# Pooled-query scores with 64 weight columns per matmul, and attention's list of work laid out anew

## Chip, cores and metric

The kernel runs on one core of one Trainium2 chip. The metric is device time in microseconds (us), the median of three runs. The engines are TensorE (PE in the rows; PEld is its weight loads, which overlap the matmuls), VectorE (DVE), ScalarE (ACT), GpSimd (POOL) and SyncE (SP), which here issues the loads and stores.

## What is computed

Attention through 32 pooled queries p, a mixture of experts in which each token goes to one expert, and a gated two-matrix layer, all in fp32:

```python
def sm_attn(qq, kk, vv):                       # scale = 1/sqrt(64)
    s = scale * np.matmul(qq, kk.transpose(0, 1, 3, 2))
    s = s - np.max(s, axis=-1, keepdims=True)
    a = np.exp(s)
    a = a / (np.sum(a, axis=-1, keepdims=True) + 1e-09)
    return np.matmul(a, vv)
p_packed = sm_attn(p, k, v)                    # 8 batches, 8 heads, 32 x 576, d = 64
out = sm_attn(q, p_packed, p_packed)           # 576 x 32: the pooled-query scores
...
logits = xn @ en.T / tau                       # 4608 rows, 8 experts
expert_idx = np.argmax(logits, axis=1)
...
h = np.maximum(x[mask] @ w1[e], 0.0)
out[mask] = gate_w[mask, None] * (h @ w2[e])
...
a = x @ w_a
b = x @ w_b
return (a * b @ w_out).astype(np.float32)
```

## The kernel before

The program has three stages, one after the other: attention (to about 196 us), the experts (lines 823 to 1135), and the gated layer with an output by quadrants (from line 1235). The change is in attention alone.

Attention goes by batch. `prep(b)` loads p, k and v; k and v come in halves of four heads (tiles `k` and `v`, three buffers each, 576 KB a load). It transposes p (L248) and k (L268), makes the scores of p with k (L298, L303), the maximum, the exponential (L323) and its sum, transposes these (L352), and adds up the pooled values with v (L369) in PSUM tile `sm`. They are scaled (L386), transposed (L394) and kept as `ppT`, two tiles with heads side by side. From them come the small products `gr` (L408 to L413). `query(b)` loads q in halves, transposes it (L453) into five tiles `qT`, and runs three windows of 192 queries by `rest`: the pooled-query scores `s2_mm` (L491), maximum (L497), subtraction (L501), exponential (L505), sum and reciprocal (L509, L510), norm (L514, on GpSimd or VectorE), transposes (L520), the products with `gr` that give norms and expert logits (L534), and two sums (L543, L548). When a batch's windows are done, `experts` chooses each token's expert by a chain of small VectorE operations (L667), in whose middle a square root is taken on GpSimd (L696).

In `s2_mm` the weights are columns of `qT` (128 rows, two positions by 64), and the moving operand is 32 or 64 columns of `ppT`. Each matmul takes 32 weight columns, so four of them fill the 128 partitions of the result: 32 matmuls a window, 24 windows. An fp32 matmul is two rows of the trace, each with a weight load.

The order of all this isn't written by hand. `Sched` gets a list of operations: the engines each may run on with a duration in us, its dependencies, a priority, the buffers it takes and frees, and `lat`, the time until others may use its result. `run` goes through it with a clock for each engine, takes among the operations that could start within 0.05 us of the earliest the one with the lowest priority number, puts it on the engine on which it would end first, and calls its code. The durations so set the order on each engine and which engine makes a copy; they are no time that anything waits. On the chip each engine runs its own list in that order and waits only for data and buffers. "D" is the load queue: SyncE's, in the order of the list. The copies out of PSUM are all line 202 (ScalarE) or 204 (VectorE).

The end of attention's plan is handed to the plan of the experts as its starting clocks; the third stage has a plan of its own.

Of the kernel before, what the change touches and what calls it, by code (L numbers as in the profile page):

```python
# [18 lines left out]
B, H, S, D, NP, E = 8, 8, 576, 64, 32, 8  # L19
# [5 lines left out]
QA = 1.5  # L25
NB = 0.6
EN0 = 5.0


class Ctx:  # L30
# [118 lines left out]
NW = CI // 3  # L149


def attention(ctx, tc, c, q, k, v, p, a_dram, pT_dram, consts, more):
    nc = tc.nc
# [50 lines left out]
            nc.vector.tensor_copy(out=out, in_=in_)  # L204

    def evict(n):
        return {"A": 0.12 + 0.0009 * n, "V": 0.1 + 0.00105 * n}

    t_en = Buf("tr")
    o_en = op({"T": 0.33}, en_mm, take=[t_en], prio=-4.0, start=EN0)  # L210
# [3 lines left out]

    def halves(x, b, h):
        return x[b, 4 * h:4 * h + 4].rearrange("(m h) (p i) d -> (h p) m (i d)", h=2, i=CI)

    def prep(b):
        lo, hi = (first[b - 1] - AHEAD, first[b] - AHEAD) if b else (-8.0, -1.0)
# [16 lines left out]
        o_p = op({"D": 0.2}, load_p, prio=at(-1.0), take=[bp], lat=2.0)  # L236
        o_k, o_v = [], []
        for l, f, pr, bb in ((o_k, load_k, -0.75, bk), (o_v, load_v, -0.45, bv)):
            for h in range(2):
                l.append(op({"D": 1.7}, f(h), deps=l[-1:], prio=at(pr) + 0.04 * h, take=[bb[h]], lat=2.0))  # L240


        def pT_mm(e):
# [42 lines left out]
        for g in range(2):  # L286
            def s1_mm(a, g=g):
                def f(e):
                    ps = psum("tr", ("s1p", b, g, a))
                    if (g, a) == (0, 0):  # L290
                        tile_("e", ("e", b), [128, CI, 2, D])

                    def w(j):
                        h = 2 * j + g
                        return T_["pT", b][:, h // 4, a, h % 4 * 32:h % 4 * 32 + 32]

                    for j in range(4):
                        nc.tensor.matmul(  # L298
                            ps[32 * j:32 * j + 32, 0:256].rearrange("q (i p) -> q i p", i=4), lhsT=w(j),
                            rhs=T_["kT", b, j][:, :, 64 * g:64 * g + 64], start=True, stop=True)  # L300
                    if a == 0:
                        for j in range(4):
                            nc.tensor.matmul(  # L303
                                ps[32 * j:32 * j + 32, 256:320], lhsT=w(j),
                                rhs=T_["kT", b, 4][:, j, 64 * g:64 * g + 64], start=True, stop=True)
                return f

            def s1_ev(a, g=g):
                def f(e):
                    s = (slice(0, 5), slice(5, 9))[a]  # L310
                    n = s.stop - s.start
                    copy(e, T_["e", b][:, s, g], T_["s1p", b, g, a][:, 0:n * D].rearrange("p (i q) -> p i q", i=n))
                return f

            def mx(e, g=g):
                T_["mx", b, g] = m = st.tile([128, 1], F32, tag="mx1", name="mx1")
                nc.vector.tensor_reduce(out=m, in_=T_["e", b][:, :, g], axis=AX.XY, op=ALU.max)
                nc.vector.tensor_scalar(out=m, in0=m, scalar1=-0.125, scalar2=None, op0=ALU.mult)

            def exp(e, g=g):  # L320
                T_["sm", b, g] = sm = st.tile([128, 1], F32, tag="sm1", name="sm1")
                ee = T_["e", b][:, :, g]
                nc.scalar.activation(  # L323
                    out=ee, in_=ee, func=AF.Exp, bias=T_["mx", b, g], scale=0.125, accum_out=sm)

            def rs(e, g=g):
                T_["rs", b, g] = r = st.tile([128, 1], F32, tag="rs1", name="rs1")
                nc.vector.tensor_scalar(out=r, in0=T_["sm", b, g], scalar1=1e-9, scalar2=None, op0=ALU.add)
                nc.vector.reciprocal(out=r, in_=r)

            f = lambda x, g=g: at(x + 0.1 * g)
            evs = []
            for a in range(2):
                t = Buf("tr")
                o = op({"T": 0.62}, s1_mm(a), deps=[o_pT] + o_kT, prio=f(0.25), take=[t] if g + a else [t, be],
                       free=[bpT] + bkT[0:4] + ([] if a else bkT[4:]))
                evs.append(op(evict(288), s1_ev(a), deps=[o], prio=f(0.25), free=[t]))
            o = op({"V": 0.86}, mx, deps=evs, prio=f(0.33))
            o = op({"A": 0.76}, exp, deps=[o], prio=f(0.37))
            T_["rso", b, g] = op({"V": 0.27}, rs, deps=[o], prio=f(0.55))  # L340
            o_e.append(o)

        def chunk(i):
# [31 lines left out]
        mms = []  # L375
        for i0, i1 in ((0, 4), (4, 8), (8, 9)):
            t = Buf("tr")
            o = op({"T": 0.11 * (i1 - i0)}, eT_mm(i0, i1), deps=o_e, prio=at(0.45 + 0.01 * i0),
                   take=[t] if i0 else [t, beT], free=[be])
            o = op(evict(128 * (i1 - i0)), eT_ev(i0, i1), deps=[o], prio=at(0.45 + 0.01 * i0), free=[t])  # L380
            mms.append(op({"T": 0.25 * (i1 - i0)}, pp_mm(i0, i1), deps=[o] + o_v + mms[-1:], prio=at(0.6 + 0.01 * i0),
                          take=[] if i0 else bs, free=[beT] + bv))

        for g in range(2):
# [42 lines left out]
            o = op({"V": 0.26}, ppx_ev, deps=[T_["rso", b, g]] + mms, prio=f(0.75), take=[bc], free=[bs[g]])  # L427
            o = op({"T": 0.11}, ppT_mm, deps=[o], prio=f(0.8), take=[t, bT], free=[bc])
            ppT_ops[b, g] = [op({"A": 0.17, "V": 0.2}, ppT_ev(a), deps=[o], prio=f(0.8), free=[t]) for a in range(2)]
            t = Buf("tr")  # L430
            o = op({"T": 0.35}, gr_mm, deps=ppT_ops[b, g], prio=f(0.9), take=[t], free=[bT])
            o = op({"V": 0.21}, gr_ev, deps=[o], prio=f(0.9), take=[bx], free=[t])
            gr_ops[b, g] = op({"A": 0.06, "V": 0.08}, m8_ev, deps=[o], prio=f(0.9), free=[t])
            c.kept[b, g] = op({"D": 0.4}, keep, deps=ppT_ops[b, g], prio=f(1.0), free=[bT], lat=2.0)

    x_ops = {}
# [1 line left out]
    def query(b):  # L438
# [2 lines left out]
        at = lambda x: first[b] + x  # L441
        o_q = []
        for h in range(2):
            o_q.append(op({"D": 1.7}, lambda e, h=h: nc.sync.dma_start(
                out=turn("q", ("q", b, h))[:, :, 0:CI, :].rearrange("p m i d -> p m (i d)"), in_=halves(q, b, h)),
                prio=at(-3.2 + 0.3 * h), deps=o_q[-1:], take=[bq[h]], lat=2.0))
        o_qT, bqT = [], []
        for x in range(5):
            def qT_mm(e, x=x):
# [24 lines left out]
    def rest(b, w, o_qT, bqT, before):  # L474
# [10 lines left out]
        def s2_mm(e):  # L485
            ps = psum("sm", ("s2", t))[:, 0:384].rearrange("p (i j k) -> p i j k", i=3, j=4)
            for j in range(4):
                for i, n in runs:
                    for o in range(0, 128, 32):
                        pT = T_["ppT", b, o // 64][:, j]  # L490
                        nc.tensor.matmul(  # L491
                            ps[o:o + 32, i - 3 * w:i - 3 * w + n, j], lhsT=T_["qT", b, i // 2][:, j, o:o + 32],
                            rhs=pT if n == 2 else pT[:, i % 2, :].unsqueeze(1), start=True, stop=True)

        def mx(e):
# [51 lines left out]
        def add(e):  # L547
# [2 lines left out]
        B_ = {n: Buf(n) for n in ("a", "an", "sq", "sm")}  # L550
        f = lambda x: 1.5 * t + x
        used = sorted({i // 2 for i, _ in runs})
        o = op({"T": 0.95}, s2_mm, deps=[o_qT[x] for x in used] + ppT_ops[b, 0] + ppT_ops[b, 1], prio=f(0),
               take=[B_["sm"]], free=[bqT[x] for x in used] + [T_["bppT", b, g] for g in range(2)])
        o = op({"V": 0.46}, mx, deps=[o], prio=f(0))
        o = op({"V": 0.47}, sub, deps=[o], prio=f(0), take=[B_["a"]], free=[B_["sm"]])
        o = op({"A": 0.43}, exp, deps=[o], prio=f(0))
        o = op({"V": 0.72}, total, deps=[o], prio=f(0.2))
        o = op({"V": 0.47} if t >= NW * B - 2 else {"P": 0.9, "V": 0.47}, norm, deps=[o], prio=f(0.2),
               take=[B_["an"]], free=[B_["a"]], bias={"V": NB})  # L560
        tr = Buf("tr")
        o = op({"T": 0.33}, aT_mm, deps=[o], prio=f(0.5), take=[tr], free=[B_["an"]])
        o_T = op(evict(384), aT_ev, deps=[o] + before[:1], prio=f(0.5), take=[] if w else [T_["baT", b]], free=[tr])
        x = Buf("x")
        o = op({"T": 0.8}, x_mm, deps=[o_T, gr_ops[b, 0], gr_ops[b, 1]], prio=f(0.7), take=[x],
               free=[T_["baT", b], T_["bgr", b, 0], T_["bgr", b, 1]])
        o_d = op({"A": 0.15, "V": 0.1}, dots, deps=[o], prio=f(0.8), free=[x])
        o = op({"V": 0.5}, sq, deps=[o], prio=f(0.8), take=[B_["sq"]], free=[x, B_["an"]])
        o = op({"V": 0.46}, add, deps=[o], prio=f(1.5), free=[B_["sq"]])
        x_ops[b] = x_ops.get(b, []) + [o_d, o]  # L570
        return o_T

# [99 lines left out]
def experts(nc, c, pool, b, psum):  # L672
# [36 lines left out]
    def g():  # L709
# [1151 lines left out]
```

## Time and profile before

| | us |
|---|---|
| median of 3 runs | 1387.64 |
| lowest and highest | 1387.16, 1387.8 |
| the profiled execution | 1386.53 |
| its span, first to last instruction | 1384.8 |

| engine | busy us | share of the span |
|---|---|---|
| TensorE matmuls | 1333.1 | 96% |
| TensorE weight loads | 1212.8 | 88% |
| VectorE | 799.1 | 58% |
| ScalarE | 589.7 | 43% |
| GpSimd | 106.9 | 8% |

The shares are means over stages that differ: the second and third stage keep TensorE full, attention doesn't. Matmuls overlap, so a busy TensorE isn't one at its peak. A gap that is put down to "issue" is one in which the engine waited for nothing that the profile shows. Windows are in us from the first instruction.

### The profile page before, as it was taken

Reading aid. Unit: us, or ns where it says so; the run is one execution under the profiler, and the core shown is the slowest. Engines: PE = TensorE matmul, PEld = TensorE weight load, DVE = VectorE, ACT = ScalarE, POOL = GpSimd, SP = SyncE. Lnnn points to the kernel's source line nnn. Section 1 sums busy time; section 2 is a strip of 40 time slices with the busy share of each in tenths; the row PEclk is TensorE's granted clock in tenths of the full one; section 3 lists DMA queues with packets and bytes.
Section 4 is the critical chain, followed back from the end, with each engine's and each line's share of the span. In section 5 each row is a group of like instructions: output and inputs, shape, how many; then the busy total and the mean of one; then the engine's idle time right before and its main releaser. Section 6 shows DMA issues by size and latency. Waiting matters only on the chain. (4 is left out here: it accounts for less than half of the span.)

```text
span 1384.8 us, 28211 instructions
## 1 busy us (share of the span) xinstructions
PE 1333.1 (96%) x11031; PEld 1212.8 (88%) x11031; DVE 799.1 (58%) x1644; ACT 589.7 (43%) x1212; POOL 106.9 (8%) x235
## 2 busy tenths in 40 slices
PE   7988879999999999999999999999999999999997
PEld 5766768999999999899999998999999989999996
DVE  4877875666766664888563446344634463444342
ACT  4655533444544444555442344234423442343232
POOL 1111210101001010000010001000100010001001
PEclk9999999999999999999999999999999999999999
DMA  7777446888676843777765566556765665556552
GB/s 266 232 253 244 155 154 203 278 265 286 227 248 197 282 148 131 256 257 255 256 196 162 158 204 199 161 158 201 209 161 159 193 209 162 158 167 199 161 158 66
DMA packets 169277, 278.14 MB, mean 201 GB/s; under 512 B 16936, under 2 KB 68520, under 8 KB 169136
## 3 DMA queue, kind: packets, MB, share of 16 engines
q1 hardware_dynamic: 162704, 257.35, 60.3%
q0 software_dynamic: 6272, 18.88, 3.9%
q8 instruction: 90, 1.47, 0.4%
q14 instruction: 51, 0.42, 0.1%
q10 hardware_dynamic: 160, 0.02, 0.0%
HBM read 219.04 MB, written 57.15 MB: 199 GB/s over the span
## 5 line engine op out<-in xcount | busy, mean ns | idle before, releaser
L1438 DVE TENSOR_TENSOR s<-s,s 128x384 f32<-128x384 f32 x324 | 176.7, 555 | 341.8 <-ACT s L1574 339.2
L760 PE MATMUL pb<-xq,wq 128*128 128x384 f32 x504 | 170.1, 338 | 1.9 <-ACT s L1574 0.7
L1687 PE MATMUL o<-oh,gh 128*128 128x512 f32 x432 | 170.1, 394 | 1.6 <-ACT osb L1707 1.6
L760 PE MATMUL pa<-xq,wq 128*128 128x384 f32 x504 | 169.6, 336 | 2.0 <-DVE s L1438 2.0
L1688 PE MATMUL o<-ol,gh 128*128 128x512 f32 x432 | 170.4, 394 | 0.0
L1689 PE MATMUL o<-oh,gl 128*128 128x512 f32 x432 | 170.4, 394 | 0.0
L762 PE MATMUL pa<-xq,wq 128*128 128x384 f32 x504 | 170.2, 338 | 0.0
L761 PE MATMUL pb<-xq,wq 128*128 128x384 f32 x504 | 170.1, 337 | 0.0
L762 PE MATMUL pb<-xq,wq 128*128 128x384 f32 x504 | 170.1, 337 | 0.0
L761 PE MATMUL pa<-xq,wq 128*128 128x384 f32 x504 | 169.9, 337 | 0.0
L760 PE MATMUL dn<-hh,w2h 128*128 128x288 f32 x512 | 153.0, 299 | 0.0
L762 PE MATMUL dn<-hh,w2l 128*128 128x288 f32 x512 | 151.0, 295 | 0.0
L761 PE MATMUL dn<-hl,w2h 128*128 128x288 f32 x512 | 150.4, 294 | 0.0
L1574 ACT COPY s<-pa 128x384 f32<-128x384 f32 x180 | 86.5, 480 | 149.5 <-PE pa L762 149.3
L1574 ACT COPY s<-pb 128x384 f32<-128x384 f32 x180 | 86.5, 480 | 141.6 <-PE pb L762 141.5
L760 PEld LDWEIGHTS dn<-hh,w2h 128*128 128x128 f32 x512 | 96.1, 188 | 11.7 <-ACT w2h L989 5.9
L760 PEld LDWEIGHTS pb<-xq,wq 128*128 128x128 f32 x504 | 94.6, 188 | 12.1 <-ACT s L1574 1.3
L760 PEld LDWEIGHTS pa<-xq,wq 128*128 128x128 f32 x504 | 94.7, 188 | 10.4 <-DVE s L1438 2.7
L761 PEld LDWEIGHTS pb<-xq,wq 128*128 128x128 f32 x504 | 94.6, 188 | 8.4
L761 PEld LDWEIGHTS pa<-xq,wq 128*128 128x128 f32 x504 | 94.6, 188 | 7.5
L1689 PEld LDWEIGHTS o<-oh,gl 128*128 128x128 f32 x432 | 81.0, 187 | 18.8
L761 PEld LDWEIGHTS dn<-hl,w2h 128*128 128x128 f32 x512 | 96.7, 189 | 0.2 <-DVE hl L1023 0.2
(192 smaller groups left out, 2433.7 us busy)
## 6 DMA issues: line engine op xcount, KB each, us to landing
wq<-ws SPq DMA_DIRECT2D x420, 256.0 KB, 2.8
ws<-wq SPq DMA_DIRECT2D x84, 256.0 KB, 3.8
raw<-in_moe_w_dram SPq DMA_DIRECT2D x36, 512.0 KB, 6.2
rawb<-in_moe_w_dram SPq DMA_DIRECT2D x28, 512.0 KB, 9.3
k<-in_k_dram SPq DMA_DIRECT2D x16, 576.0 KB, 6.5
v<-in_v_dram SPq DMA_DIRECT2D x16, 576.0 KB, 6.5
q<-in_q_dram SPq DMA_DIRECT2D x16, 576.0 KB, 5.9
xr<-x2T SPq DMA_DIRECT2D x20, 384.0 KB, 4.3
```

The lines of the kernel that those rows point to most:

```text
L760: nc.tensor.matmul(ps, lhsT=wh, rhs=xh, start=start, stop=False, **kw)
L761: nc.tensor.matmul(ps, lhsT=wh, rhs=xl, start=False, stop=False, **kw)
L762: nc.tensor.matmul(ps, lhsT=wl, rhs=xh, start=False, stop=stop, **kw)
L1438: VT = lambda out, a, b, o: V.tensor_tensor(out=out, in0=a, in1=b, op=o)
L1574: A.copy(out=T[n, key], in_=ps[n, names_bank[key]])
L1687: nc.tensor.matmul(a, lhsT=gh[:, h, s], rhs=wh, start=first, stop=False)
L1688: nc.tensor.matmul(a, lhsT=gh[:, h, s], rhs=wl, start=False, stop=False)
L1689: nc.tensor.matmul(a, lhsT=gl[:, h, s], rhs=wh, start=False, stop=last)
```

## The change

One: `s2_mm` takes 64 weight columns per matmul, so two matmuls fill the result where four did; a window has 16 matmuls. Two: the durations in attention's list are others, and so are those of the root in `experts`. Three: the loads of k, v and q lose their dependency on the half before. They now have a fixed order among their own kind (`after`, which holds for the plan), and are held to land 4.0 us after their issue, not 2.0. Cut to its core:

```diff
+LAND = 4.0
     def evict(n):
-        return {"A": 0.12 + 0.0009 * n, "V": 0.1 + 0.00105 * n}
+        return {"A": 0.13 + 0.0009 * n, "V": 0.14 + 0.00105 * n}
...
-                l.append(op({"D": 1.7}, f(h), deps=l[-1:], prio=at(pr) + 0.04 * h, take=[bb[h]], lat=2.0))
+                l.append(op({"D": 1.9}, f(h), prio=at(pr) + 0.04 * h, take=[bb[h]], lat=LAND, after=loads.get(pr)))
+                loads[pr] = l[-1]
...
-                    for o in range(0, 128, 32):
+                    for o in range(0, 128, 64):
                         pT = T_["ppT", b, o // 64][:, j]
                         nc.tensor.matmul(
-                            ps[o:o + 32, i - 3 * w:i - 3 * w + n, j], lhsT=T_["qT", b, i // 2][:, j, o:o + 32],
+                            ps[o:o + 64, i - 3 * w:i - 3 * w + n, j], lhsT=T_["qT", b, i // 2][:, j, o:o + 64],
...
-        o = op({"T": 0.95}, s2_mm, deps=[o_qT[x] for x in used] + ppT_ops[b, 0] + ppT_ops[b, 1], prio=f(0),
+        o = op({"T": 0.6}, s2_mm, deps=[o_qT[x] for x in used] + ppT_ops[b, 0] + ppT_ops[b, 1], prio=f(0),
...
-    return [("T", 0.2, pairs, "take"), ("V", 0.16, both, "free")] + V(a) + [("P", 0.6, root, "")] + V(d), [
+    return [("T", 0.2, pairs, "take"), ("V", 0.16, both, "free")] + V(a) + [("P", 1.8, root, "")] + V(d), [
```

The other durations are of this kind: maximum 0.46 to 0.55, sum 0.72 to 0.79, exponential of the first scores 0.76 to 0.97, pooled values 0.25 to 0.13 per chunk.

What the new durations do to the order is seen on three engines. The load queue (SyncE) at the start of the program, before; `pz` is p, the number after a name tells buffers and tiles apart:

```order
L226 DMA pz0_153<-in_p_dram 128x2x64
L229 DMA k0_157<-in_k_dram 128x2x576
L233 DMA v_269<-in_v_dram 128x2x576
L226 DMA pz1_154<-in_p_dram 128x2x64
L229 DMA k1_158<-in_k_dram 128x2x576
L229 DMA k2_159<-in_k_dram 128x2x576
L233 DMA v_308<-in_v_dram 128x2x576
```

and after:

```order
L229 DMA pz0_153<-in_p_dram 128x2x64
L232 DMA k0_157<-in_k_dram 128x2x576
L232 DMA k1_158<-in_k_dram 128x2x576
L236 DMA v_270<-in_v_dram 128x2x576
L236 DMA v_285<-in_v_dram 128x2x576
L229 DMA pz1_154<-in_p_dram 128x2x64
L232 DMA k2_159<-in_k_dram 128x2x576
```

The first batch's second half of k (`k1`) has moved from behind `v` and `pz1` to directly behind the first half, and the two halves of v stand together.

VectorE in the last batch, around the root of the batch before (`r_264`; the root itself is on GpSimd, between the row that reads `ndt_261` and the row that reads `tau`), before:

```order
L690 COPY ndt_261<-tr_3842 128x81
L667 TENSOR_SCALAR r_264<-ndt_261 128x9
L509 TENSOR_REDUCE sm_3900<-as_213 128x12
L510 RECIPROCAL sm_3900<-sm_3900 128x12
L667 TENSOR_SCALAR r_264<-r_264,tau 128x9
L514 TENSOR_TENSOR an<-as_213,sm_3900 128x384
L667 RECIPROCAL r_264<-r_264 128x9
L497 TENSOR_REDUCE mx_3916<-sm 128x12
```

and after:

```order
L672 TENSOR_SCALAR r_264<-ndt_261 128x9
L672 TENSOR_TENSOR g2i<-sm_260 128x9
L514 TENSOR_REDUCE sm_3506<-as_214 128x12
L515 RECIPROCAL sm_3506<-sm_3506 128x12
L514 TENSOR_REDUCE sm_3510<-as_213 128x12
L515 RECIPROCAL sm_3510<-sm_3510 128x12
L519 TENSOR_TENSOR an<-as_214,sm_3506 128x384
L519 TENSOR_TENSOR an<-as_213,sm_3510 128x384
L672 TENSOR_SCALAR r_264<-r_264,tau 128x9
L502 TENSOR_REDUCE mx_3522<-sm 128x12
```

Two rows stood between the row ahead of the root and the row behind it; now there are seven, two norms (`an`) among them, and the last window's maximum (`mx`) stands behind them all.

Over attention VectorE gets 6 copies of kT and 6 of ppT fewer and two of eT more, with smaller exchanges, and ScalarE the reverse; one norm moves from GpSimd to VectorE.

## Rows read from the trace of the kernel before

**Rows 1.** Windows: stretch and length, busy us (instructions), granted clock, DMA share, GB/s

```profile
30.00:180.00 150.00, 131.18 (x3589) 102.58 (x3591) 121.22 (x369) 84.64 (x199) 28.30 (x27) 0.98 0.66 222
180.00:196.00 16.00, 8.07 (x179) 5.89 (x179) 10.72 (x34) 6.28 (x14) 2.62 (x2) 0.86 0.05 19
300.00:1384.00 1084.00, 1069.54 (x6107) 992.64 (x6106) 585.56 (x1082) 442.53 (x903) 63.00 (x174) 1.00 0.63 193
```

The busy columns are those of PE, PEld, DVE, ACT and POOL, here and in groups 3 and 10.

**Rows 2.** Waits, TensorE, 6 to 196 us: in total, times, longest (us)

```profile
PE sm L491 <- issue: 9.9, 6, 2.0
PE sm L369 <- issue: 3.5, 1, 3.5
PE tr L268 <- DMA k<-in_k_dram: 2.7, 3, 1.7
PE tr L303 <- issue: 1.6, 2, 0.9
```

**Rows 3.** Windows between ends of gaps; DMA view to 196 us: packets, MB, share

```profile
32.46:48.05 15.59, 15.00 (x379) 12.03 (x379) 11.87 (x31) 8.63 (x21) 1.67 (x2) 1.00 0.90 291
48.05:53.03 4.98, 3.00 (x127) 2.15 (x128) 4.60 (x15) 2.00 (x5) 0.83 (x1) 1.00 1.00 324
72.60:85.22 12.62, 9.02 (x253) 7.64 (x253) 9.79 (x30) 5.05 (x12) 3.46 (x3) 1.00 0.87 324
...
q8 instruction: 33, 0.54, 1.2%
```

**Rows 4.** Timeline, TensorE near 182 us: start, length, work, idle before

```profile
182.40 0.67 PE L491 MATMUL sm<-ppT,qT 128*32 128x64 f32 x40 [2.04 <-issue]
```

**Rows 5.** Groups to 196 us (busy us, mean ns); timeline of three of them

```profile
L491 PE MATMUL sm<-ppT,qT 128*32 128x64 f32 (+1 forms) x1536 | 23.8, 209 | 10.6 <-issue 9.9 <-ACT qT L202 0.5
L62 PE MATMUL enps<-ident,e 8*128 8x8 f32 x4 | 0.6, 255 | 0.0
...
178.49 0.91 PE L491 MATMUL sm<-ppT,qT 128*32 128x64 f32 x64
8.09 0.59 PE L62 MATMUL enps<-ident,e 8*128 8x8 f32 x4
166.01 0.92 PE L534 MATMUL x<-gr,aT 128*64 128x136 f32 x12
```

A tile such as 128\*32 is the rows and columns of the array that the weights fill.

**Rows 6.** Waits, VectorE, 30 to 196 us

```profile
DVE mx L497 <- PE sm L491: 6.0, 5, 1.8
DVE pc L386 <- PE sm L369: 3.6, 2, 3.2
...
DVE r L667 <- POOL r L696: 2.6, 3, 1.1
```

**Rows 7.** Timeline, load queue and TensorE at the start

```profile
2.33 0.46 SPq L233 DMA_DIRECT2D v<-in_v_dram  x1
3.35 1.29 SPq L229 DMA_DIRECT2D k<-in_k_dram  x2
11.45 2.79 PE L268 MATMUL tr<-ident,k 128*128 128x128 f32 x12 [1.72 <-DMA k<-in_k_dram]
```

**Rows 8.** Timeline, last root and the first matmul of the experts

```profile
185.54 1.79 POOL L696 TENSOR_TENSOR r<-r,half 128x9 f32<-128x9 f32 x1
187.37 0.23 DVE L667 TENSOR_SCALAR r<-r,tau 128x9 f32<-128x9 f32 x1 [1.11 <-POOL r L696]
187.51 0.55 DVE L514 TENSOR_TENSOR an<-as,sm 128x384 f32<-128x384 f32 x1
196.15 0.61 PE L760 MATMUL up<-ath,zh 128*128 128x288 f32 x1
```

**Rows 9.** Groups, VectorE to 196 us

```profile
L204 DVE COPY kT<-tr 128x512 f32<-128x512 f32 x10 | 6.8, 682 | 6.4 <-PE tr L268 6.4
L204 DVE COPY ppT<-tr 64x128 f32<-64x128 f32 x16 | 4.5, 288 | 4.3 <-PE tr L394 3.2 <-ACT ppT L202 0.8
```

**Rows 10.** Windows, behind the gap of 3.5 us

```profile
85.00:90.00 5.00, 4.77 (x68) 4.02 (x70) 1.66 (x6) 2.12 (x6) 0.00 (x0) 0.66 0.35 105
```

More of the change, by code (lines that the diff above doesn't have):

```diff
@@ L216, in halves @@
         return x[b, 4 * h:4 * h + 4].rearrange("(m h) (p i) d -> (h p) m (i d)", h=2, i=CI)
+    loads = {}
     def prep(b):
@@ L234, in load_v @@
                 out=tile_("v", ("v", b, h), [128, 2, CI, D]).rearrange("p m i d -> p m (i d)"), in_=halves(v, b, h))
-        o_p = op({"D": 0.2}, load_p, prio=at(-1.0), take=[bp], lat=2.0)
+        o_p = op({"D": 0.2}, load_p, prio=at(-1.0), take=[bp], lat=LAND)
         o_k, o_v = [], []
@@ L334, in prep @@
                 t = Buf("tr")
-                o = op({"T": 0.62}, s1_mm(a), deps=[o_pT] + o_kT, prio=f(0.25), take=[t] if g + a else [t, be],
+                o = op({"T": 0.46}, s1_mm(a), deps=[o_pT] + o_kT, prio=f(0.25), take=[t] if g + a else [t, be],
                        free=[bpT] + bkT[0:4] + ([] if a else bkT[4:]))
[L337 to L340, printed above, removed]
+                evs.append(op(evict(256 if a else 320), s1_ev(a), deps=[o], prio=f(0.25), free=[t]))
+            o = op({"V": 0.94}, mx, deps=evs, prio=f(0.33))
+            o = op({"A": 0.97}, exp, deps=[o], prio=f(0.37))
+            T_["rso", b, g] = op({"V": 0.3}, rs, deps=[o], prio=f(0.55))
             o_e.append(o)
@@ L377, in prep @@
             t = Buf("tr")
-            o = op({"T": 0.11 * (i1 - i0)}, eT_mm(i0, i1), deps=o_e, prio=at(0.45 + 0.01 * i0),
+            o = op({"T": 0.12 * (i1 - i0)}, eT_mm(i0, i1), deps=o_e, prio=at(0.45 + 0.01 * i0),
                    take=[t] if i0 else [t, beT], free=[be])
             o = op(evict(128 * (i1 - i0)), eT_ev(i0, i1), deps=[o], prio=at(0.45 + 0.01 * i0), free=[t])
-            mms.append(op({"T": 0.25 * (i1 - i0)}, pp_mm(i0, i1), deps=[o] + o_v + mms[-1:], prio=at(0.6 + 0.01 * i0),
+            mms.append(op({"T": 0.13 * (i1 - i0)}, pp_mm(i0, i1), deps=[o] + o_v + mms[-1:], prio=at(0.6 + 0.01 * i0),
                           take=[] if i0 else bs, free=[beT] + bv))
@@ L426, in prep @@
             bc = Buf("pc")
-            o = op({"V": 0.26}, ppx_ev, deps=[T_["rso", b, g]] + mms, prio=f(0.75), take=[bc], free=[bs[g]])
-            o = op({"T": 0.11}, ppT_mm, deps=[o], prio=f(0.8), take=[t, bT], free=[bc])
-            ppT_ops[b, g] = [op({"A": 0.17, "V": 0.2}, ppT_ev(a), deps=[o], prio=f(0.8), free=[t]) for a in range(2)]
+            o = op({"V": 0.34}, ppx_ev, deps=[T_["rso", b, g]] + mms, prio=f(0.75), take=[bc], free=[bs[g]])
+            o = op({"T": 0.13}, ppT_mm, deps=[o], prio=f(0.8), take=[t, bT], free=[bc])
+            ppT_ops[b, g] = [op({"A": 0.26, "V": 0.29}, ppT_ev(a), deps=[o], prio=f(0.8), free=[t]) for a in range(2)]
             t = Buf("tr")
             o = op({"T": 0.35}, gr_mm, deps=ppT_ops[b, g], prio=f(0.9), take=[t], free=[bT])
-            o = op({"V": 0.21}, gr_ev, deps=[o], prio=f(0.9), take=[bx], free=[t])
-            gr_ops[b, g] = op({"A": 0.06, "V": 0.08}, m8_ev, deps=[o], prio=f(0.9), free=[t])
+            o = op({"V": 0.28}, gr_ev, deps=[o], prio=f(0.9), take=[bx], free=[t])
+            gr_ops[b, g] = op({"A": 0.15, "V": 0.14}, m8_ev, deps=[o], prio=f(0.9), free=[t])
             c.kept[b, g] = op({"D": 0.4}, keep, deps=ppT_ops[b, g], prio=f(1.0), free=[bT], lat=2.0)
@@ L443, in query @@
         for h in range(2):
-            o_q.append(op({"D": 1.7}, lambda e, h=h: nc.sync.dma_start(
+            o_q.append(op({"D": 1.9}, lambda e, h=h: nc.sync.dma_start(
                 out=turn("q", ("q", b, h))[:, :, 0:CI, :].rearrange("p m i d -> p m (i d)"), in_=halves(q, b, h)),
-                prio=at(-3.2 + 0.3 * h), deps=o_q[-1:], take=[bq[h]], lat=2.0))
+                prio=at(-3.2 + 0.3 * h), take=[bq[h]], lat=LAND, after=loads.get("q")))
+            loads["q"] = o_q[-1]
         o_qT, bqT = [], []
@@ L552, in rest @@
         used = sorted({i // 2 for i, _ in runs})
-        o = op({"T": 0.95}, s2_mm, deps=[o_qT[x] for x in used] + ppT_ops[b, 0] + ppT_ops[b, 1], prio=f(0),
+        o = op({"T": 0.6}, s2_mm, deps=[o_qT[x] for x in used] + ppT_ops[b, 0] + ppT_ops[b, 1], prio=f(0),
                take=[B_["sm"]], free=[bqT[x] for x in used] + [T_["bppT", b, g] for g in range(2)])
[L555 to L559, printed above, removed]
+        o = op({"V": 0.55}, mx, deps=[o], prio=f(0))
+        o = op({"V": 0.55}, sub, deps=[o], prio=f(0), take=[B_["a"]], free=[B_["sm"]])
+        o = op({"A": 0.53}, exp, deps=[o], prio=f(0))
+        o = op({"V": 0.79}, total, deps=[o], prio=f(0.2))
+        o = op({"V": 0.55} if t >= NW * B - 2 else {"P": 0.84, "V": 0.55}, norm, deps=[o], prio=f(0.2),
                take=[B_["an"]], free=[B_["a"]], bias={"V": NB})
         tr = Buf("tr")
-        o = op({"T": 0.33}, aT_mm, deps=[o], prio=f(0.5), take=[tr], free=[B_["an"]])
+        o = op({"T": 0.38}, aT_mm, deps=[o], prio=f(0.5), take=[tr], free=[B_["an"]])
         o_T = op(evict(384), aT_ev, deps=[o] + before[:1], prio=f(0.5), take=[] if w else [T_["baT", b]], free=[tr])
         x = Buf("x")
-        o = op({"T": 0.8}, x_mm, deps=[o_T, gr_ops[b, 0], gr_ops[b, 1]], prio=f(0.7), take=[x],
+        o = op({"T": 0.86}, x_mm, deps=[o_T, gr_ops[b, 0], gr_ops[b, 1]], prio=f(0.7), take=[x],
                free=[T_["baT", b], T_["bgr", b, 0], T_["bgr", b, 1]])
-        o_d = op({"A": 0.15, "V": 0.1}, dots, deps=[o], prio=f(0.8), free=[x])
-        o = op({"V": 0.5}, sq, deps=[o], prio=f(0.8), take=[B_["sq"]], free=[x, B_["an"]])
-        o = op({"V": 0.46}, add, deps=[o], prio=f(1.5), free=[B_["sq"]])
+        o_d = op({"A": 0.18, "V": 0.14}, dots, deps=[o], prio=f(0.8), free=[x])
+        o = op({"V": 0.55}, sq, deps=[o], prio=f(0.8), take=[B_["sq"]], free=[x, B_["an"]])
+        o = op({"V": 0.54}, add, deps=[o], prio=f(1.5), free=[B_["sq"]])
         x_ops[b] = x_ops.get(b, []) + [o_d, o]
```

## Prediction

> **What bounds the kernel now.** I first cut the span into stretches, to see which stage the edits lie in [rows 1]. From 300 us to the end TensorE is busy 1069.54 of 1084 us: the two MoE stages are bound by it, and neither their code nor, but for one group of twelve matmuls that swaps places, their order is touched. All that the change does happens before 196 us, in attention, and whatever that stage gains or loses is carried to the end one for one. Inside attention, from 30 to 180 us, TensorE is busy 131.18 of 150 us and VectorE 121.22: two engines that feed each other, neither full. After 180 us comes a thin end, where TensorE is busy 8.07 of 16 us.
>
> Next I read what TensorE waited for [rows 2]. Three of the four rows say "issue": 9.9 us in 6 gaps ahead of the pooled-query scores (L491), 3.5 us in one gap ahead of L369, 1.6 us in two ahead of L303. Together that is 15.0 us in nine gaps in which no semaphore is named, so nothing in the kernel's own dependencies explains them. The windows that run from the end of one gap to the end of another explain them [rows 3]: TensorE's instructions (weight loads and matmuls, the two counts in brackets) are 379 + 379, 127 + 128 and 253 + 253, that is 758, 255 and 506, each a little under 768, 256 and 512, and a few records can be missing. So a gap comes three, one or two borders after the last, where a border is the end of 256 instructions, and the row of the instruction queue has the other half: 33 pieces and 0.54 MB in attention, 16 KB each, which for 256 instructions is 64 bytes apiece. TensorE runs out of code at some of these borders. These three windows have the DMA engines busy for 0.90, 1.00 and 0.87 of their time: the piece of code stands behind loads of k, v and q. The last gap lies inside one scores window, 2.04 us ahead of its last 40 matmul rows [rows 4], after 180 us, where the DMA engines are busy 0.05 of the time [rows 1]; so a block that passes quickly can be enough.
>
> The Trainium skill, "Runtime: NRT & Kernel Launch", section "Instruction fetch mechanics", has the same 16 KiB pieces of 256 instructions, and calls the crossing of a border "mostly hidden". By that sentence halving the instructions would save nothing here; the trace has 24 pieces whose crossing is hidden and nine that cost 15.0 us, and by that sentence the fetch term below would be 0.
>
> **The change, part by part.**
>
> *Fetch.* The scores are 1536 matmul rows, two for each matmul, with as many weight loads [rows 5]. With 64 weight columns half of both go: 768 + 768 = 1536 instructions, 6 blocks of 256 out of 33. From 30 to 180 us TensorE ran 3589 + 3591 instructions [rows 1], 28 blocks; 150 us less the 15.0 of gaps is 4.8 us of work to a block. The same work in 27 blocks for 33 makes that 5.9, and a fetch of the same lateness has 1.1 us more. Taken from the nine gaps: those of L303 (0.8 each) go, the longest (3.5) becomes 2.4, and the six of L491 (mean 1.65) leave 6 x 0.55 = 3.3; 5.7 us, times 27/33 for the fewer borders, is 4.7. TensorE so gains 15.0 - 4.7 = 10.3 us. The ends are 15 us (no gap is left) and nothing (the next rival).
>
> *The matmuls themselves.* Now the 64 rows of a window run in 0.91 us at a mean of 0.21 each, so they start 11 ns apart: four column tiles side by side make a round in 44 ns. The nearest row for the cost of weights is L62, four loads of 128 columns with 8 moving columns: 0.59 us for all at a mean of 0.255, so 0.112 us apart for 128 columns, or 0.056 for 64 [rows 5]. L534 has 64-column weights in two halves of the array: 12 rows in 0.92 us, 0.056 us apart, with 136 moving columns, more than the whole array could stream one after the other, so two tiles do run at once. After the change a window has 32 rows in 16 rounds of two. If a round is bound by its weights it lasts 0.056 us: 0.90 us, and 0.21 for the last to drain, 1.11 us against 0.91. If it is bound by the streaming, as the 44 ns rounds may be, it stays at 0.91; if the 11 ns were a price per instruction, it would fall to 0.56. I take 1.11, since L62 is the one row where weights alone set the pace: +0.20 us, times 24 windows +4.8 us of TensorE, with ends of -8.4 and +4.8. So the edit by itself makes the matmuls slower; what it brings is fewer instructions.
>
> *How much of TensorE's time reaches the end.* VectorE waited for the scores 6.0 us and for L369 3.6 us after the first batch [rows 6]; 9.6 of the 15.0 us of gaps came out as idle VectorE, 0.64. I take that share for both terms: fetch -6.6, matmuls +3.1.
>
> *Head.* The list of work now has both halves of the first k ahead of v on the load queue. Before, the second half stood behind a v and a pz: issued at 3.35 us, and TensorE waited 1.72 us for it until 11.45 [rows 7]. Issued at 2.33, where the v stood, and with the same 8.1 us from issue to use, it is there at 10.4; with one load less ahead of it (576 KB at the 324 GB/s of [rows 3], 1.8 us, an estimate) at 8.6. That is 1.0 to 2.8 us; the evictions behind it are a chain of their own, so I take -2.0. It reaches the end, since everything in the first batch hangs on it; what would be late next is the v pair, which the first L369 needs.
>
> *The root on GpSimd.* The plan held it to take 0.6 us; it takes 1.79 [rows 8]. VectorE stood waiting for it 2.6 us in three places [rows 6], 1.11 of it in the last, on the path to the end of the stage. In the new order seven instructions, two norms among them, stand between the step before the root and the step after, against two. Two norms at 0.55 us with two sums and two reciprocals cover 1.8. I take the last wait whole and half of the others: -1.9 (ends 0 and -2.6). The cost is that the last window's maximum now stands behind both norms; it has to wait for its matmuls in any case.
>
> *VectorE's load.* The plan now gives a VectorE eviction 0.04 us more. By the order, VectorE loses 6 copies of kT at 0.682 and 6 of ppT at 0.288 [rows 9] and small ones come and go: 4.0 us less in all, and ScalarE gets as much. VectorE is not full, so I count a quarter: -1.0 (ends 0 and -4.0).
>
> *The rest of the layout,* other durations and a landing time of 4.0 us for 2.0, moves most rows of the stage and adds none. I put it at zero, since no row of before can price an order that was not run. Its lower end: VectorE is idle 28.8 us from 30 to 180, of which 9.6 are counted above, so at the most 19 us. Its upper end is the second rival.
>
> *Clock.* Behind the gap of 3.5 us, in which TensorE stood still, the granted clock of 85 to 90 us is 0.66 in the mean [rows 10]: part of the stretch ran at the lower of its two levels, 1.2 GHz. If that gap shrinks some of it may come back; I leave it out, as a margin.
>
> **Sum:** -6.6 + 3.1 - 2.0 - 1.9 - 1.0 = -8.4 us. The profiled execution took 1386.53 us (span 1384.8 and 1.7 around it), 1.1 below the median of 1387.64 and just outside the three runs; against itself the sum gives 1378.1, against the median 1379.2. I predict 1379.2.
>
> **Rivals.**
>
> 1. *The gaps stay.* The refill of code stands behind loads, not behind a clock; the change leaves the bytes as they are and puts loads side by side that stood apart, two of k and two of v. If each border then waits for one more load of 1.5 us, the 1.1 us won per block is gone. For it: the busy data queues of [rows 3]. Against it: the gap of [rows 4], with hardly any load about. Without the fetch term: 3.1 - 2.0 - 1.9 - 1.0 = -1.8, 1385.8 us. By the sentence of the Trainium skill quoted above the same comes out.
>
> 2. *The preparation of a batch comes too late: slower.* The plan now lets a load land 4.0 us after its issue, not 2.0, so it may lay the transposes of k, the first scores and the pooled values of a batch 2.0 us later, behind other work on TensorE. If the queries of that batch then wait for it, that is up to 2.0 us for each of 7 batches, +14: -8.4 + 14 = +5.6, 1393.2 us. It turns the sign from 1.2 us per batch, and leaves the band of no change from 1.6. Against it: TensorE waited for k 2.7 us in three places only [rows 2], and the new queue order asks for loads no later.
>
> 3. *The layout pays more.* Durations that fit the chip let VectorE wait less everywhere: half of the 19 us above, -9.5 more, 1369.7 us. For it: the root shows what a wrong number costs. Against it: an order made from durations is still fixed, and the code gaps fall where no plan sees them.
>
> **How the numbers follow.** The forecast, from 1373 (matmuls at their price of before, -3.1, and VectorE's load whole, -3.0) to 1384.8: 0.52. Rival 1: 0.20. Rival 2: 0.15. Rival 3: 0.13. A measurement of this kernel can tell 0.2%, 2.8 us, from no change: faster (below 1384.9) is the forecast and rival 3 with a little of rival 1, 0.67; within 0.2% is most of rival 1, 0.19; slower 0.14. The range goes from 1367 (rival 3 with the matmuls at their price of before, -3.1) to 1389 (rival 1 with the upper ends of head and root, +1.0 and +1.9). What lies outside is most of rival 2 and the far end of rival 3.
>
> **What would show it.** Right: about 27 pieces of code in attention, not 33, and fewer than nine gaps without a releaser, 5 to 8 us in all; a scores window of 32 rows in about 1.1 us; the wait for k that ended at 11.45 us gone or ended by 10; no VectorE wait over 0.5 us for the root. The first MoE matmul, at 196.15 us before [rows 8], at about 188. Wrong: gaps that sum to 12 us or more, a window at 0.9 us or less, or new waits of TensorE for k, v or q.

## The result, and the profile after

The changed kernel takes 1370.98 us (median of four runs, 1369.52 to 1371.9) where the kernel before took 1387.4 in the same comparison: a ratio of 0.9885, interval 0.9868 to 0.9902, 16.4 us less. In a second comparison, on another chip, it was 1372.78 against 1388.5: 0.989, interval 0.9867 to 0.9912. I had said 1379.2, 8.4 us less. The measured time is inside my range (1367 to 1389), below the band of the forecast itself (1373 to 1384.8). The direction and the main mechanism held, the size was half.

The first matmul of the experts, at 196.15 us before [rows 8], now starts at 182.83, so 13.3 us come from attention, the only stage that was touched. From there to the end it is 1186.7 us after and 1188.6 before; over all the kernels below this rest lies between 1185.0 and 1188.7 with hardly a change in its order, so its 1.9 us are within the spread between executions.

TensorE's waits from 6 to 196 us after (in total, times, longest, us) answer [rows 2]; the row of the instruction queue and the windows answer [rows 3] and [rows 1], with the same columns:

```profile
PE tr L525 <- DVE sm L672: 3.0, 1, 3.0
PE sm L373 <- issue: 1.8, 1, 1.8
PE tr L525 <- DVE an L519: 1.6, 1, 1.6
...
PE tr L307 <- issue: 0.5, 1, 0.5
...
PE sm L496 <- issue: 0.4, 1, 0.4
```

```profile
q8 instruction: 27, 0.44, 1.0%
```

```profile
30.00:180.00 150.00, 137.63 (x2969) 107.55 (x2967) 121.72 (x385) 88.49 (x213) 30.32 (x28) 0.99 0.65 213
```

The lines are five further down than before (L491 is L496, L369 is L373, L520 is L525). 33 pieces of code have become 27. The gaps in which no semaphore is named, 15.0 us in nine, are 2.7 us in three (1.8, 0.5 and 0.4), and TensorE is busy 137.63 of the 150 us where it was 131.18, VectorE 121.72 where it was 121.22.

The scores themselves, a group to 184 us and one window (start, length), answer [rows 5]:

```profile
L496 PE MATMUL sm<-ppT,qT 128*64 128x64 f32 (+1 forms) x768 | 28.0, 224 | 1.6 <-ACT qT L203 0.8 <-DVE as L506 0.4 <-issue 0.4
```

```profile
127.75 1.13 PE L496 MATMUL sm<-ppT,qT 128*64 128x64 f32 x32
```

A window has 32 rows for 64 and takes 1.13 us for 0.91: half the instructions, and 0.22 us more. In the trace of this window the weight loads start in pairs, the two of a pair 7 ns apart and the pairs 55 to 59 ns, whether 32 or 64 columns move, while the matmuls start unevenly; so here the weights set the pace, as I had taken it.

The start, the timeline of TensorE, answers [rows 7]:

```profile
6.86 4.22 PE L272 MATMUL tr<-ident,k 128*128 128x128 f32 x20
11.01 0.93 PE L302 MATMUL tr<-kT,pT 128*32 128x256 f32 x8
```

The 20 transposes of k run without a stop, and the first scores of p with k start at 11.01 us; before, the wait for k lasted to 11.45 and those scores started at 14.17.

### The profile page after: what moved, and what is told of

Its sections match the earlier page's. It is cut to its first block, busy times and chain, and to the rows that moved or that the text cites. A ratio compares the mean times of both kernels' runs of the same rounds, so it can differ in the third digit from the quotient of the medians.

```text
span 1369.5 us, 26692 instructions
## 1 busy us (share of the span) xinstructions
PE 1335.0 (97%) x10263; PEld 1214.9 (89%) x10263; DVE 790.8 (58%) x1635; ACT 591.9 (43%) x1222; POOL 106.5 (8%) x234
```

## The experiments

All ratios are to runs of the kernel before on the same chip. The gaps are those over 0.3 us ahead of an instruction of TensorE that names no semaphore, from 6 us to the first matmul of the experts. "k scores" is the start of the first matmul of the k scores. "Clock" is the mean granted clock over the whole span, averaged over the runs.

| kernel | set | pieces | gaps, us | k scores, us | clock | median, us | ratio (interval) |
|---|---|---|---|---|---|---|---|
| before | 1 | 33 | 15.1 | 14.17 | 0.9892 | 1388.38 | 1 |
| 64 columns alone | 1 | 27 | 4.5 | 14.47 | 0.9929 | 1378.27 | 0.9936 (0.991 to 0.9963) |
| after, with 32 columns | 1 | 33 | 13.8 | 10.91 | 0.9919 | 1385.19 | 0.9967 (0.9948 to 0.9987) |
| after, loads as before | 1 | 27 | 8.5 | 14.92 | 0.9932 | 1379.93 | 0.9944 (0.9923 to 0.9965) |
| before, new loads alone | 1 | 33 | 16.1 | 11.31 | 0.9909 | 1384.0 | 0.9966 (0.9948 to 0.9984) |
| after, again | 2 | 27 | 1.8 | 11.29 | 0.993 | 1372.78 | 0.989 (0.9867 to 0.9912) |
| before, light loads | 2 | 33 | 1.3 | 14.07 | 0.993 | 1371.17 | 0.988 (0.9853 to 0.9907) |
| after, shifted by half a piece | 2 | 27 | 3.5 | 11.12 | 0.9937 | 1375.63 | 0.991 (0.9889 to 0.993) |
| after, last norm first | 2 | 27 | 4.0 | 10.58 | 0.9948 | 1368.24 | 0.9855 (0.9832 to 0.9879) |
| the same, again | 3 | 27 | 2.4 | 10.72 | 0.9958 | 1369.59 | 0.9864 (0.9838 to 0.989) |
| after, landing in 2.0 us | 3 | 27 | 6.4 | 11.60 | 0.9928 | 1379.73 | 0.9932 (0.9904 to 0.9959) |
| after, root at 0.6 us | 3 | 27 | 0.4 | 11.32 | 0.9942 | 1371.76 | 0.9871 (0.9847 to 0.9896) |

Kernels of a set ran beside the same runs of before. Gaps and k scores are those of one profile of each kernel; the clock and median of before are those of the 28 runs of set 1. In sets 2 and 3, of 11 runs each, its medians were 1388.5 and 1389.08. Differences in us below are differences of ratios times 1388. For after once more I had expected 0.9885 and gaps of 2.7 to 3.3 us; it has 0.989 and 1.8.

**64 columns alone, in the old order.**

```diff
-                    for o in range(0, 128, 32):
+                    for o in range(0, 128, 64):
...
-                            ps[o:o + 32, i - 3 * w:i - 3 * w + n, j], lhsT=T_["qT", b, i // 2][:, j, o:o + 32],
+                            ps[o:o + 64, i - 3 * w:i - 3 * w + n, j], lhsT=T_["qT", b, i // 2][:, j, o:o + 64],
```

> The kernel before with one edit: 64 weight columns per matmul in the pooled-query scores; list, durations and loads are those of before, so every engine keeps its order. Theory A (the two terms of my forecast that hang on this edit, fetch -6.6 and matmuls +3.1): 27 pieces of code where there were 33, gaps without a releaser down from 15.0 us to about 5, a scores window of 32 rows in 1.1 us, and 3.5 us off: ratio 0.9975. Theory B (a border waits for whatever loads stand ahead, so gaps don't shrink with the instructions): gaps stay at 12 us or more, the slower matmuls remain, +3 us: 1.002. Theory C (all that was measured hangs on the code gaps, the layout is worth nothing): the whole -16 us, 0.988.

Measured: 0.9936, 8.9 us less, between theories A and C. TensorE's waits in it:

```profile
PE sm L369 <- issue: 3.6, 2, 3.4
PE tr L520 <- DVE eb L667: 2.9, 1, 2.9
PE tr L268 <- DMA k<-in_k_dram: 2.4, 2, 1.4
...
PE tr L408 <- issue: 0.6, 1, 0.6
...
PE tr L956 <- issue: 0.5, 1, 0.5
```

The pieces and the gaps are as theory A has them (27, and 4.5 us left), and the six gaps ahead of the scores are gone. But the time fell by 8.9 us and not by 3.5: the gaps were seen rightly, and what I made of them was not. Theory B falls.

**The new list with 32 columns.** The first diff the other way round, on the kernel after.

> The kernel after with one edit undone: 32 weight columns per matmul again, in the new order, so 1536 rows of scores and 33 pieces of code. Theory A (columns and layout add up as in my forecast, layout a little more): the gaps without a releaser are back at 10 to 15 us, the scores window at 0.9 us, and the time is 5 to 10 us under the kernel before: ratio 0.993 to 0.996. Theory B (the layout pays nearly all of it, the fetch next to nothing): 12 us or more under before: below 0.9915. Theory C (the layout pays nothing by itself): 1.000.

Measured: 0.9967, 4.6 us less, just above the range of theory A and with an interval that reaches into it. The gaps are back at 13.8 us. So the two parts nearly add up: 8.9 and 4.6 are 13.5 of the 15.3 to 16.0 us (0.989 and 0.9885) of both. The profiled execution of this kernel was one of the longer ones (1386.29 us), with a granted clock of 0.95 from 30 to 180 us against 0.98 in the profile of before. In it the experts start at 198.09 us, later than the 196.15 of before, so the 4.6 us are read from the runs and not from this trace. Its window:

```profile
30.00:180.00 150.00, 132.49 (x3412) 100.00 (x3413) 109.42 (x342) 84.56 (x201) 28.12 (x27) 0.95 0.63 208
```

**The loads apart.** Two kernels: after with the old planning of its loads, and before with the new one alone.

```diff
-                l.append(op({"D": 1.9}, f(h), prio=at(pr) + 0.04 * h, take=[bb[h]], lat=LAND, after=loads.get(pr)))
+                l.append(op({"D": 1.7}, f(h), deps=l[-1:], prio=at(pr) + 0.04 * h, take=[bb[h]], lat=2.0))
```

and the same for q, and `LAND` at 2.0 for p; in the other kernel the reverse.

> The kernel after with the loads of k, v and q planned as before: the second half of each pair depends on the first, 1.7 us each, held to land after 2.0 us, no order of their own. Durations, root and 64 columns are those of after. Theory A (the loads part is worth what the head gained, 3.2 us by the first matmul of the k scores, 11.01 us where it was 14.17): 3 us slower than the kernel after, ratio to before 0.9905, and the second half of k waits again behind a v. Theory B (the landing time is what lets the plan fit the chip in every batch): 6 us or more slower than after, 0.993 or above, with new waits of TensorE for k, v or q. Theory C (the loads part is worth nothing): as after, 0.988.

> The kernel before with the loads part alone: the loads of k, v and q in fixed order among their kind, 1.9 us each, held to land after 4.0 us; old durations, old root, 32 columns. Theory A: the first batch starts 3 us earlier and the rest is as before, code gaps of about 15 us among it: 3 us off, ratio 0.998. Theory B (a landing time of 4.0 us moves the work of every batch, and TensorE waits less): 6 us or more off, 0.996 or below. Theory C (4.0 us put the preparation of a batch too late): slower than before.

Measured: 0.9944 and 0.9966. New loads in the old list bring 4.7 us, as much as the whole new list with 32 columns (4.6). And without them, the new durations with 64 columns (0.9944) are no better than 64 columns alone (0.9936). So of the layout it is the loads that can be seen to pay; the other durations, the root's among them, bring nothing that these times can tell from zero. That isn't the same as nothing: the kernel with the old loads has 4.0 us more of gaps in its profile than that with 64 columns alone (8.5 and 4.5), which can hide a gain of that size. By the time the first of the two is theory B, but its waits for loads are those of the first batch; the second lies between theories A and B. The start of the k scores follows the loads in all kernels: 14.1 to 14.9 us with the old ones, 10.6 to 11.6 with the new ones, about 3 us. Undoing the loads in the kernel after costs more than that, about 7.5 us (0.9944 against 0.989), and its trace has 8.5 us of gaps for 1.8 to 2.7, besides the wait for k that is back.

**Landing time alone.** After with `LAND = 2.0`; the fixed order of the loads stays.

> The kernel after with the loads held to land 2.0 us after their issue, as in the kernel before; their fixed order, 1.9 us each, all other durations and the 64 columns stay. Theory A (the fixed order is the whole worth of the loads part, by an earlier second half of k in the first batch): first matmul of the k scores at 11.0 us as in after, time within 2 us of after, ratio 0.989 to 0.9905. Theory B (the landing time pays too, since the plan no longer lays work ahead of its data): TensorE waits for k, v or q in batches behind the first, 3 us or more above after, ratio 0.991 or above.

Measured: 0.9932, 5.8 us above after (0.989), with intervals that just overlap (0.9904 and 0.9912). By the time that is theory B, but hardly by its mechanism. TensorE's waits, the largest, and those for a load:

```profile
PE sm L373 <- issue: 3.7, 2, 2.8
PE tr L272 <- issue: 2.7, 1, 2.7
PE tr L356 <- ACT e L327: 2.7, 3, 1.3
...
PE tr L272 <- DMA k<-in_k_dram: 0.7, 1, 0.7
PE tr L458 <- DMA q<-in_q_dram: 0.4, 1, 0.4
```

The waits for k and q are 1.1 us, where after has none. What grew more are the gaps, from 1.8 or 2.7 us to 6.4, about 4 of the 5.8 us.

**Where the borders fall.** After with 64 small transposes ahead of everything, at a time when TensorE has no data; the order of all that follows is that of after on every engine.

```diff
+    pad = psum.tile([128, 512], F32, tag="tr", name="pad")
+    for i in range(64):
+        nc.tensor.transpose(pad[:32, 0:8], c.ident[:E, 0:32], c.ident[:E, :E])
```

> The kernel after with 64 transposes of 32 columns ahead of everything, in the time in which TensorE has no data: 128 more instructions, half a piece of code, so all borders lie half a block earlier in the same work. Theory A (which borders cost is a matter of where they fall; 27 pieces cost between 2.7 us, in the kernel after, and 8.5 us, with the old loads): the gaps come elsewhere and sum to 3 to 8 us, and the time is 0 to 5 us above the kernel after, ratio 0.9885 to 0.992. Theory B (the new order leaves few gaps, wherever the borders lie): 2.5 to 3.5 us of gaps, time within 1.5 us of after.

Measured: 0.991, 2.8 us above after, with intervals that overlap. The start of the k scores is the same (11.12), and the gaps stand elsewhere: 1.2 us at 34 us and 2.3 at 58 us, where after had 0.4 at 60, 1.8 at 122 and 0.5 at 130. That is theory A in kind: the same work in the same order has other gaps when the borders move by half a piece, though the difference in size, 1 to 2 us of gaps, is near what the times can tell.

**What a piece of code stands behind.** The kernel before, in its old order with 32 columns and 33 pieces, but with a ninth of the bytes in each load of k, v and q from the third batch on. The buffers keep old rows (v gets three of its own for that), so what those batches compute is left out.

```diff
+    few = lambda b: CI if b < 2 else 1
...
-                out=turn("k", ("k", b, h))[:, :, 0:CI, :].rearrange("p m i d -> p m (i d)"), in_=halves(k, b, h))
+                out=turn("k", ("k", b, h))[:, :, 0:few(b), :].rearrange("p m i d -> p m (i d)"), in_=halves(k, b, h)[:, :, 0:few(b) * D])
```

> The kernel before, in its own order with 32 columns and 33 pieces of code, but from the third batch on each load of k, v and q brings one ninth of its bytes (the buffers keep old rows, so the results of those batches are left out). Theory A (a piece of code stands behind the bytes of k, v and q): of the seven gaps without a releaser behind 50 us, 12.7 us in all, less than 3 us are left, and the time is 10 us or more under the kernel before, ratio 0.993 or below. Theory B (a piece comes late because its block passes quickly, whatever the loads do): those gaps stay at 10 us or more, and the time falls by no more than the waits for k and q, 3 us: 0.998.

Measured: 0.988, 16.7 us less, from nothing but fewer bytes. The instruction queue, TensorE's waits and the windows from 30 to 180 us:

```profile
q8 instruction: 33, 0.54, 1.2%
```

```profile
PE tr L522 <- POOL an L516: 2.8, 5, 1.4
PE tr L270 <- DMA k<-in_k_dram: 2.3, 2, 1.5
PE tr L522 <- DVE eb L669: 2.2, 1, 2.2
...
PE sm L493 <- issue: 1.3, 1, 1.3
```

```profile
30.00:180.00 150.00, 136.79 (x3748) 105.76 (x3747) 131.74 (x402) 88.71 (x211) 30.83 (x29) 0.96 0.32 97
```

The same 33 pieces are fetched, the DMA engines are busy 0.32 of the time and not 0.66 [rows 1], and of nine gaps one is left, 1.3 us. The experts start at 181.63 us, 14.5 us earlier than before, and 13.8 us of gaps are gone. The gap that is left is at 165.5 us, inside a scores window, as the gap of [rows 4] was, so a block that passes quickly can still be enough by itself. Theory A is shown, theory B falls: the refill of code comes late because of the bytes of k, v and q. Whether it stands in line behind them or shares the DMA engines with them, these runs don't tell apart. So an engine waits not only for data and buffers, but for its code as well. The Trainium skill, "Runtime: NRT & Kernel Launch", section "Instruction fetch mechanics", calls the crossing of a border "mostly hidden"; in this kernel that holds with light loads (1.3 us for 33 pieces) and not with the full ones (15.1 us).

**The root at its old price.** After with 0.6 us for the root in the plan.

```diff
-... + [("P", 1.8, root, "")] + ...
+... + [("P", 0.6, root, "")] + ...
```

> The kernel after with the root on GpSimd planned at 0.6 us again, as before; all else stays. Theory A (the term of my forecast: VectorE stands for the root again and the last of these waits reaches the end): waits of VectorE for POOL's r of 2 us or more in all, the kernel 1 to 2 us slower than after, ratio 0.990 to 0.9905. Theory B (the wait only moves: in after TensorE stands 3.0 to 3.7 us for a norm that VectorE does late, so what the root gives is lost there): the waits are back and the time is that of after, 0.989, within 0.001.

Measured: 0.9871, not slower than after (0.989). VectorE's waits for the root in it, from 6 to 196 us:

```profile
DVE r L672 <- POOL r L701: 5.2, 5, 2.0
```

In the kernel after that row is 0.2 us. The longest of the five, 2.0 us, lies behind the first matmul of the experts; the four in attention are 3.2 us, a little more than the 2.6 of [rows 6]. So the waits are back and the time isn't longer, as theory B has it. That they cost nothing isn't shown: this profile has 0.4 us of gaps where the two of after have 2.7 and 1.8, which can hide a cost of 1 to 2 us. In the last stretch, from the last copy of `ndt` (the row ahead of the root) to the first matmul of the experts, none of these profiles has a gap. It takes 13.04 us here, 12.07 and 11.85 in the two profiles of after, so there the old price does cost about 1 us.

**Last norm first, a kernel that goes beyond the change.** In the kernel after the last norm stands behind a row of smaller steps of VectorE, and TensorE waits for it at the end of the stage:

```profile
180.18 0.52 PE L525 MATMUL tr<-ident,an 128*128 128x128 f32 x3 [2.98 <-DVE sm L672]
181.27 1.63 PE L539 MATMUL x<-gr,aT 128*64 128x136 f32 x12 [0.57 <-ACT aT L203]
182.83 0.61 PE L765 MATMUL up<-ath,zh 128*128 128x288 f32 x1
```

```diff
+        last = 9.0 if t == NW * B - 1 else 0.0
...
-        o = op({"V": 0.79}, total, deps=[o], prio=f(0.2))
+        o = op({"V": 0.79}, total, deps=[o], prio=f(0.2) - last)
-... norm, deps=[o], prio=f(0.2),
+... norm, deps=[o], prio=f(0.2) - last,
```

> The kernel after with one change in its list: sum and norm of the last window of all come ahead of the products and sums of the windows before it, on VectorE. In the trace of after TensorE waits 2.98 us at 180.18 us for that norm, which stands behind ten smaller steps. Theory A (this wait is on the path to the first matmul of the experts): the wait falls under 1 us and the kernel is 2 us faster than after, ratio 0.987. Theory B (something else is late next, the weights of the first expert or its rows): the first matmul of the experts stays where it was, and the ratio with it, 0.9885.

> The kernel with sum and norm of the last window ahead of the steps of the windows before it, once more, for a second profile and more times. Theory A (the wait of 3 us at the end of attention was on the path): ratio 0.985 to 0.987 again, TensorE's wait for the last norm under 1 us, a first matmul of the experts ahead of that of after by 2 us where the gaps without a releaser are alike. Theory B (the better time was chance of the runs): 0.989.

Measured: 0.9855 and 0.9864. The same place in the second profile:

```profile
177.63 0.52 PE L525 MATMUL tr<-ident,an 128*128 128x128 f32 x3 [1.73 <-DVE an L519]
178.71 0.92 PE L539 MATMUL x<-gr,aT 128*64 128x136 f32 x12 [0.57 <-ACT aT L203]
179.56 0.40 PE L766 MATMUL up<-ath,zh 128*128 128x288 f32 x1
```

The wait is 1.73 us here, more than I had expected, and 0.62 in the first profile, against 2.98 and 3.7 in the two of after, and the experts start at 179.56 (182.15 in the first profile, whose gaps were 4.0 us). The waits for `hl` a little behind sum to 3.2 us in both profiles, to 1.8 in those of after. Both medians, 1368.24 and 1369.59, are under those of after, 1370.98 and 1372.78, but the intervals overlap: the gain on after, some 3 us, is not proven by the times. The stretch from the last copy of `ndt` to the experts has it, 9.02 and 8.84 us for 12.07 and 11.85; the gain on before is proven, 19 to 20 us.

## Why the prediction was right, and half the size

**Fetch: mechanism right, size nearly.** 15.0 us of gaps were to leave 4.7; the kernel after has 2.7 and 1.8, and the nine profiles with 27 pieces have between 0.4 and 8.5, in the mean 3.8. The three with 33 pieces and full loads have 13.8 to 16.1. Fewer borders alone, at the same price each, would have left 27/33 of 15.1, 12.3 us. Rival 1 (the gaps stay) had the cause right, as the light loads show, and the consequence wrong: with half the instructions in the scores most refills arrive in time. That this is because a block lasts longer fits, but no run tests it apart.

**The matmuls: right.** Weight-bound windows of 1.11 us were predicted, 1.13 are there, +0.22 x 24 = +5.3 us for +4.8. The groups as a whole, 28.0 us for the 23.8 of [rows 5], make it +4.2: a window that a gap cuts in two takes longer, 0.79 and 0.36 us in one of before.

**The step that failed: how much of TensorE's time reaches the end.** I took 0.64, because VectorE's waits for L491 and L369 came to 9.6 us and the gaps to 15.0 [rows 2, 6]. That set two sums side by side without following one gap to the end. The kernel with 64 columns alone has the answer: TensorE lost 10.6 us of gaps there (15.1 to 4.5) and got 5.3 us more of matmuls, 5.3 net (6.4 by the groups), and the first matmul of the experts starts at 189.58 for 196.15, 6.6 us earlier. The whole net arrives. By the windows TensorE is busy 139.04 us from 30 to 180 where it was 131.18 [rows 1]:

```profile
30.00:180.00 150.00, 139.04 (x2996) 109.29 (x2985) 126.79 (x381) 87.84 (x205) 30.07 (x29) 0.98 0.65 220
```

And nothing has taken the place of the gaps: TensorE's idle times over 0.3 us that do name a semaphore, from 6 us to the experts, sum to 13.6 us before and 13.0 there. TensorE set the pace, and its time passes whole. VectorE's waits are no measure of the share. The two rows that I divided come to 3.8 us in that kernel, but in the kernel after, which has fewer gaps still, to 7.6 us (waits of VectorE, 30 to 196 us):

```profile
DVE mx L502 <- PE sm L496: 4.6, 9, 1.0
DVE pc L390 <- PE sm L373: 3.0, 3, 1.6
```

With a share of 1 the edit gives -5.3 us by itself (8.9 were measured, 5.1 to 12.5 by the interval), and -12.4 + 5.3 = -7.1 in the kernel after, where I had -6.6 + 3.1 = -3.5.

**Head: right, too small.** -2.0 within 1.0 to 2.8; the first k scores start 2.9 to 3.2 us earlier, and the new loads alone brought 4.7 (2.2 to 7.2 by the interval).

**Root and VectorE's load: not borne out by the times, and open.** I had -1.9 and -1.0; all new durations together, load and root among them, gave 0.9944 for 0.9936 (old loads, 64 columns), and the old price of the root gave 0.9871 for 0.989. No worth shows in the times, but the gaps of these profiles differ by as much as the terms. Of the root one part can be read from the traces. I was right that its last wait of 1.11 us lay on the path: behind it VectorE has no wait up to the last norm, and TensorE waits for that norm (the row names `eb`, which ended 0.04 us after it). In the kernel before:

```profile
192.46 0.55 DVE L514 TENSOR_TENSOR an<-as,sm 128x384 f32<-128x384 f32 x1
193.15 0.87 PE L520 MATMUL tr<-ident,an 128*128 128x128 f32 x3 [2.94 <-DVE eb L667]
```

What I had wrong is that the path would be shorter without it. In the new order VectorE runs 29 instructions behind the last copy of `ndt` up to that norm, for 21 before, and TensorE still waits 2.98 us for it. From that copy to the experts it is 11.39 us before and 12.07 and 11.85 after: the change as a whole didn't shorten this end.

**Clock: left out, and open.** The mean granted clock over the span is 0.9892 and 0.9896 in the runs of before (sets 1 and 2) and 0.9955 and 0.993 in those of after (first comparison and set 2); the kernel with light loads, whose gaps went with no change to the list, has 0.993 too. Within the runs of before alone the time falls by 0.9 us for each 0.001 of clock in sets 1 and 2 and by 1.3 in set 3, as fitted lines have it. At 0.9 the 3.4 to 6.3 thousandths are 3 to 6 us. This is a correlation: a run with longer gaps may be both slower and more often at 1.2 GHz, so part of it may be the gaps again. That the clock pays by itself was not shown. Nor does it follow the gaps from profile to profile: from 30 to 180 us it is 0.96 in the one with light loads, which has one gap, and 0.98 in that of before, which has nine. I had kept it as a margin with 0.66 in one stretch behind a gap [rows 10].

**The sum again,** with the measured terms: fetch -12.4, matmuls +5.3, head -3.2, root and load taken as 0: -10.3; with the clock -13 to -16. 15.3 and 16.0 were measured. So the missing 7 to 8 us are the share of 0.64 and the smaller gaps (3.6 us), the head (1.2) and the clock with what goes along with it (3 to 6), less the 2.9 us of root and load, of which the times show nothing. That the parts come near the whole rests on the clock term, which is a correlation.

**The rivals.** Rival 2 (preparation too late) did not come: no wait for k, v or q is left. Rival 3 gave nearly the right time, 1369.7, but not shown to be for its reason: the durations by themselves brought nothing that can be told. Of what I named as signs, the pieces (27), the window (1.1 us), k (no wait left) and the root (0.2 us) came as said; the gaps were to be 5 to 8 us and were 2 to 3, and the experts were to start at about 188 us and start at 182.8.

**Open.** Whether a landing time of 4.0 us has fewer gaps by itself. The six profiles with it and 27 pieces have 0.4 to 4.0 us, the three with 2.0 us 4.5 to 8.5; but with 33 pieces it brought no fewer (16.1 in the old list and 13.8 in the new, 15.1 before), and half a piece of shift moves the gaps as well.

## What to carry to other kernels

Gaps of TensorE that name no semaphore and stand 256 instructions, or a multiple of that, apart are code that arrives late; here they cost 15 us behind busy data loads and 1.3 us behind light ones, so fewer instructions and fewer bytes are two cures for the same thing. To see how much of an engine's time reaches the end, don't divide another engine's waits by its gaps: look whether the engine has any long waits for data, and if it has few (here 13 of some 190 us), count its time whole. Before you count a wait that will go as time won, read the next wait behind it on the engine that sets the pace: here the root's wait went, and TensorE's wait for the last norm stayed at 3 us, since the norm stood behind more work.

## What the runs showed of the hardware

Cutting the loads from the third batch on to a ninth of their bytes, with the order of the instructions as it was, was worth 16.7 us, as much as the whole change. I had expected 10 or more. With 64 weight columns a window of 32 rows takes 1.13 us, a row's mean is 224 ns for 209, and the instructions of two column tiles overlap, so halving the rows costs 0.22 us and not a halving or a doubling. And the kernel before ran between 1382.79 and 1396.15 us in 28 runs on one chip, where three runs had lain within 0.64 us: a spread of three runs says little.
